# The seven-term product of the second pass over pairs of batches

## The chip, the cores and the metric

The kernel runs on one core of a Trainium2 chip. The core has a matrix engine, TensorE (PE; its weight loads are shown apart as PEld), and VectorE (DVE), ScalarE (ACT), GpSimd (POOL) and SyncE (SP, which issues nearly all transfers). The metric is the device time of one execution in microseconds, lower is better.

## The reference

Two stages follow each other. The first is attention over 8 batches of 8 heads, with 512 local tokens (each sees the tokens within 32 places, and all global ones) and 32 global tokens (each sees all). The second is a feed-forward block over the 8 x 544 token rows that come out of it:

```
h = x @ w_in                                  # x: 4352 x 512, w_in: 512 x 2048
sp = np.maximum(h, 0.0) + np.log1p(np.exp(-np.abs(h)))
g = h * erf(sp)
return (g @ w_out).astype(np.float32)         # w_out: 2048 x 512
```

## The kernel before

The hidden width of 2048 doesn't fit the on-chip memory at once, so the block runs in two passes of 1024 hidden columns each. Pass one stores its part of each product with w_out (`part`); pass two adds it (tile `pr`) to its own. A pass goes through nine chunks of tokens: chunks 0 to 7 are the 512 local tokens of a batch, chunk 8 all 256 global tokens. `ORDER` (L61) has the order: in pass two 7, 0, 1, ..., 6, 8, chunk 7 first, since its x stays from pass one.

**Numbers in two parts.** Every float32 operand is split into a high and a low part (names ending in h and l: `xh`/`xl`, `winh`/`winl`, `gh`/`gl`). A product is three matmuls: high by high, high by low, low by high. A split is a rounding copy (high part) and a subtraction (low part).

**A chunk.** `fetch_x` loads x from DRAM into `rx`, of which there is one buffer. The splits make its parts. A product with w_in gives h in the PSUM tile `h`, which is copied to `hs`. `gate` (L1185) takes four `hs` tiles at a time: on ACT a table load, four softplus, a table load and four erf (both into `sp`); then, per tile, sp times hs, the rounding copy `gh` and the subtraction `gl`. There are five buffers each of `gh` and `gl`. `project` (L1230) multiplies these by w_out into four PSUM tiles `op`; the result plus `pr` goes to `os` (two buffers) and out.

**The seven-term product.** In pass two, chunks 0 to 6 don't compute x @ w_in directly. `seven_x` (L1060) and `quad` (L1108) take it as a product of 2 x 2 blocks and need seven block products in place of eight (the scheme of Strassen and Winograd). Here the token dimension is halved: a block of x has 256 tokens of one batch, so each matmul has 256 columns. The block sums of w_in (`s0` to `s3`) are made once in pass two by `sums` (L1016); four sums of blocks of x, t1 to t4, are made for every batch, in `tx`. The `plus` steps on DVE (L1141) build two `hs` tiles out of the seven products: one copy and seven additions of 256 columns, from PSUM. Two products share a PSUM bank.

**The order of the work.** All of it is recorded as operations with a key, and `Program.schedule` (L147) plans them: it goes through a model of the engines, takes the lowest key that is ready, chooses among the engines that an operation allows, and so fixes the order of the instructions on each engine. The numbers at L30 to L36 and L64 set the keys. On the chip each engine runs its instructions strictly in that order. PSUM holds two `h` banks and six `a` banks; the latter hold the `op` tiles and every second `h` bank of a seven-term product.

Of the kernel before, what the change touches and what calls it, by code (L numbers as in the profile page):

```python
# [11 lines left out]
F32 = mybir.dt.float32  # L12
# [8 lines left out]
P = 128  # L21
# [10 lines left out]
QLEAD, VLEAD, RLEAD, XLEAD = (2.5517, -0.209), (2.5481, -1.9553), -1.589, (0.7497, -0.3176, 3.5675)  # L32
GOFF, POFF = (2.9757, 11.7735, 13.7388), (4.2669, 10.7934, 9.0092)
WIN, WOUT = (-7.7104, -6.1993, 11.4311, 3.451), (12.8759, 6.0818, 5.4762, 5.2864)
LATE = (59.1852, 78.8604, 52.8757, 44.675, 64.9113, 64.4638, 52.382, 80.1539)
BIAS, AHEAD = 0.8855, 14.1627  # L36

HARM = 1.719
# [19 lines left out]
MLEAD = 0.8021  # L58

SPAN = 7  # L60
ORDER = ((0, 1, 2, 3, 4, 5, 6, 8, 7), (7, 0, 1, 2, 3, 4, 5, 6, 8))  # L61
PLAIN, MERGE = 0, 0
SEVEN = (0, 1, 2, 3, 4, 5, 6)
SUMS = (84.0754, 85.2555)  # L64

TURN, GTURN = 22, 6
GSPLIT = 3
# [244 lines left out]
def kernel(  # L312
# [795 lines left out]
    def quad(c, q, X, key):  # L1108
# [47 lines left out]
        plus(3, [], ((1, L), 0, (1, L)))  # L1156
        return list(zip(H, S))

    def unit(ps, c, v, X, key):
# [24 lines left out]

    def gate(ps, c, us, key, first):  # L1185
# [10 lines left out]
        add(  # L1196
            {"ACT": 2.5 + 1.29 * (ps == 0) + 1.12 * len(us)},
            key,
            erf,
            [TAB, *(x[0] for x in us)],  # L1200
            [x[1] for x in us],
        )
        G = []
        for v, (Hb, SPb) in zip(first, us):
            nm = f"{ps}_{c}_{v}"
            k = key + 0.01 * v
            GH = mbuf([P, SL], F32R, f"gh_{nm}", "gh", 5)
            GL = mbuf([P, SL], F32R, f"gl_{nm}", "gl", 5)
            add({"DVE": 0.62, "POOL": 1.35}, k, lambda e, SPb=SPb, Hb=Hb: vec[e].tensor_tensor(SPb.ap, SPb.ap, Hb.ap, ALU.mult), [Hb], [SPb])
            add({"DVE": 0.35, "ACT": 0.56}, k, lambda e, SPb=SPb, GH=GH: copy(e, GH.ap, SPb.ap), [SPb], [GH])  # L1210
            add({"DVE": 0.62, "POOL": 1.35},
                k,
                lambda e, SPb=SPb, GH=GH, GL=GL: vec[e].tensor_tensor(GL.ap, SPb.ap, GH.ap.bitcast(F32), ALU.subtract),
                [SPb, GH],
                [GL],
            )
            G.append((GH, GL))
        return G

    def store_out(c, t, O):  # L1220
        if c < B:
# [8 lines left out]
    def project(ps, c, G, key, order=range(NU), OP=None, final=True):  # L1230
        nt = 4 if c < B else 2
        fresh = OP is None
        if fresh:
            OP = [psum_a([P, DM], f"op_{ps}_{c}_{t}") for t in range(nt)]

        def mm2(t, u):
            WH, WL = W["out", ps, u]
            for a in range(2):
                GH, GL = G[2 * u + a] if c < B else G[u]
                s0 = P * t + (0 if c < B else 256 * a)  # L1240
                lh, ll = (g.ap[:, s0 : s0 + P] for g in (GH, GL))
                first = fresh and u == order[0] and a == 0
                last = final and u == order[-1] and a == 1
                pe(OP[t].ap, lh, WH.ap[:, a, :], start=first, stop=False)
                pe(OP[t].ap, lh, WL.ap[:, a, :], start=False, stop=False)
                pe(OP[t].ap, ll, WH.ap[:, a, :], start=False, stop=last)

        for t in range(nt):
            if c == B:
# [67 lines left out]
    for ps in range(2):  # L1317
        for c in ORDER[ps]:
            n = NV if c < B else NU
            if ps == 1 and c == SPAN:  # L1320
                for i in range(5, 2 * NU):
                    load_late(i)
                for u in range(2):
                    sums(u, SUMS[u])
            if ps == 1 and c in SEVEN[PLAIN:]:
                X = seven_x(c, s - XLEAD[2])
                G = {}
                for i in range(0, NU, 2):
                    us = [x for q in range(i, i + 2) for x in quad(c, q, X, s + 2 * q)]
                    vs = [v for q in range(i, i + 2) for v in (q, q + NU)]  # L1330
                    G.update(zip(vs, gate(ps, c, us, s + 2 * i + 4 + GOFF[2], vs)))
                project(ps, c, G, s + 4 + POFF[2], (0, 2, 1, 3))
                s += n
                continue
            span = c == SPAN
            X = kept[0] if span and ps else load_x(ps, c, s - XLEAD[ps])
            us = [unit(ps, c, v, X, s + v) for v in range(n)]
            last = ps == 1 and c == ORDER[1][-1]
            G = []
            for a, z in ((0, 2), (2, 3), (3, 4)) if last else [(i, i + 4) for i in range(0, n, 4)]:  # L1340
                G += gate(ps, c, us[a:z], s + z + GOFF[ps], range(a, z))
            OP = project(ps, c, G, s + 4 + POFF[ps], range(NU), kept[1] if span and ps else None, not span or ps == 1)
            if span:
                kept = X, OP
            s += n
# [84 lines left out]
```

## Time and profile before

| | |
|---|---|
| Median of 3 runs | 903.62 us (903.03 to 903.79) |
| The profiled execution, its own time | 905.85 us |
| Its span (first to last instruction) | 904.0 us, so 1.85 us lie around it |
| PE busy | 891.8 us (99%), 9289 matmuls |
| DVE / ACT / POOL busy | 674.5 us (75%) / 522.2 us (58%) / 244.2 us (27%) |
| Pass two | from about 504 us to the end |

A matmul in flight overlaps the next one, and its end is modelled. So a busy PE says only that PE had work, and what a matmul costs is read from a long unbroken run of them: the time from the first start to the next piece's start, over the count. The granted clock of TensorE is 1.00 all through, its level of 2.4 GHz.

### The profile page before, as it was taken

The page shows a single profiled execution, that of the slowest core. Times are in us where ns is not written, and L with a number is a line of the kernel's source. Part 1 is how long each engine was busy: PE and PEld are TensorE (multiplying, and loading weights), DVE is VectorE, ACT ScalarE, POOL GpSimd, SP SyncE. Part 2 cuts the span into 40 slices and gives each one's busy share as a digit, 9 for nine tenths or more (in the row PEclk, how much of TensorE's full clock was granted, in tenths as well). Part 3 has the DMA queues.
Part 4 walks back from the last instruction along what each step waited for, and adds up shares of the span by engine and source line. Part 5 has one row for each costly group of instructions (what it writes and reads, how often), then busy time and mean ns, then how long its engine had stood idle before and what let it go on. Part 6 is the DMA issues. An engine that isn't in the chain of part 4 may idle for free.

```text
span 904.0 us, 22910 instructions
## 1 busy us (share of the span) xinstructions
PE 891.8 (99%) x9289; PEld 736.2 (81%) x9300; DVE 674.5 (75%) x1567; ACT 522.2 (58%) x962; POOL 244.2 (27%) x181
## 2 busy tenths in 40 slices
PE   9999999999999999999999999999999999999998
PEld 5677777777777777778898888988999899999986
DVE  3899797667757676773985898898878787787553
ACT  4778882855557466663756664655454545453540
POOL 0002242312533115330510324354222323233100
PEclk9999999999999999999999999999999999999999
DMA  9997988889798898975452210321324152303034
GB/s 349 349 314 232 301 256 241 303 242 319 261 257 276 252 307 269 278 239 164 131 136 95 115 47 1 71 63 33 70 71 94 57 115 60 96 24 95 1 94 116
DMA packets 93209, 153.53 MB, mean 170 GB/s; under 512 B 11952, under 2 KB 55728, under 8 KB 93104
## 3 DMA queue, kind: packets, MB, share of 16 engines
q1 hardware_dynamic: 92912, 151.81, 53.9%
q8 instruction: 73, 1.20, 0.6%
q10 hardware_dynamic: 192, 0.26, 0.1%
q14 instruction: 32, 0.26, 0.1%
HBM read 111.41 MB, written 40.63 MB: 168 GB/s over the span
## 4 chain that ended last, share of the span: by engine, by line
PE 80%; DVE 12%; DMA 4%; issue 2%; ACT 1%; POOL 1%; SPq 0%; DVEq 0%; POOLq 0%
PE op L350 34%; PE h L350 32%; PE s L350 5%; DVE raw_in L371 2%; PE o L350 2%; PE spare L350 2%; PE ga L350 2%; DMA rx<-xsc 2%; DVE xl L371 2%; DVE hs L371 1%; PE go L350 1%; PE s L351 1%; DVE gl L371 1%; DVE xh L371 1%; DVE sp L371 1%
## 5 line engine op out<-in xcount | busy, mean ns | idle before, releaser
L350 PE MATMUL op<-wouth,gh 128*128 128x512 f32 x544 | 217.5, 400 | 0.6 <-issue 0.6
L350 PE MATMUL op<-woutl,gh 128*128 128x512 f32 x544 | 212.4, 390 | 0.0
L350 PE MATMUL op<-wouth,gl 128*128 128x512 f32 x544 | 212.1, 390 | 0.0
L371 POOL TENSOR_TENSOR sp<-sp,hs 128x512 f32<-128x512 f32 x78 | 113.0, 1471 | 271.6 <-ACT sp L352 271.6
L350 PE MATMUL h<-xh,winh 128*128 128x512 f32 (+1 forms) x464 | 164.6, 355 | 0.6 <-DVE hs L371 0.5
L350 PE MATMUL h<-xh,winl 128*128 128x512 f32 (+1 forms) x464 | 162.2, 350 | 0.0
L350 PE MATMUL h<-xl,winh 128*128 128x512 f32 (+1 forms) x464 | 162.0, 349 | 0.0
L350 PEld LDWEIGHTS op<-wouth,gh 128*128 128x128 f32 x544 | 102.2, 188 | 27.3 <-issue 6.4
L350 PEld LDWEIGHTS op<-wouth,gl 128*128 128x128 f32 x544 | 102.1, 188 | 22.2
L350 PEld LDWEIGHTS op<-woutl,gh 128*128 128x128 f32 x544 | 102.3, 188 | 19.0 <-issue 0.5
L353 ACT ACT_TABLE_LOAD x90 | 115.5, 1283 | 2.3 <-PEq L1417 0.7
L352 ACT ACTIVATE gh<-sp 128x512 fp32r<-128x512 f32 x85 | 52.0, 631 | 92.8 <-PE op L350 84.4
L371 DVE TENSOR_TENSOR gl<-sp,gh 128x512 fp32r<-128x512 f32 x105 | 96.5, 939 | 7.2 <-ACT gh L352 6.4
L350 PEld LDWEIGHTS h<-xh,winh 128*128 128x128 f32 x464 | 87.7, 189 | 17.1 <-issue 2.7
L352 ACT ACTIVATE hs<-h 128x512 f32<-128x512 f32 (+1 forms) x68 | 36.9, 543 | 110.4 <-PE h L350 110.0
L350 PEld LDWEIGHTS h<-xl,winh 128*128 128x128 f32 x464 | 87.8, 189 | 12.0
L350 PEld LDWEIGHTS h<-xh,winl 128*128 128x128 f32 x464 | 87.7, 189 | 11.7
L371 DVE TENSOR_TENSOR hs<-h,hs 128x256 f32<-128x256 f32 x196 | 76.5, 417 | 11.8 <-PE h L350 7.7
L352 ACT ACTIVATE sp<-hs 128x512 f32<-128x512 f32 x136 | 74.9, 620 | 0.7 <-DVE gl L371 0.4
L352 ACT ACTIVATE sp<-sp 128x512 f32<-128x512 f32 x136 | 74.8, 620 | 0.4
L371 POOL TENSOR_TENSOR gl<-sp,gh 128x512 fp32r<-128x512 f32 x31 | 46.4, 1505 | 80.2 <-ACT gh L352 41.9
L371 DVE CAST gh<-sp 128x512 fp32r<-128x512 f32 x51 | 32.9, 652 | 43.2 <-PE op L350 42.8
(179 smaller groups left out, 1538.9 us busy)
## 6 DMA issues: line engine op xcount, KB each, us to landing
vb<-in_vB_dram SPq DMA_DIRECT2D x32, 650.0 KB, 5.7
qk<-in_qk_dram SPq DMA_DIRECT2D x30, 656.0 KB, 7.0
rx<-xsc SPq DMA_DIRECT2D x52, 256.0 KB, 5.2
va<-in_vA_dram SPq DMA_DIRECT2D x32, 390.0 KB, 5.8
px<-tp SPq DMA_DIRECT2D x84, 128.0 KB, 4.8
pt<-px SPq DMA_DIRECT2D x21, 512.0 KB, 5.5
raw_in<-in_w_in_dram SPq DMA_DIRECT2D x16, 512.0 KB, 7.3
xsc<-xT SPq DMA_DIRECT2D x32, 256.0 KB, 5.5
```

Source lines behind the costliest of these rows:

```text
L350: pe = lambda n, *a, **k: pinned(nc.tensor.matmul(n, *a, **k))
L351: tr = lambda *a, **k: pinned(nc.tensor.transpose(*a, **k))
L352: act = lambda *a, **k: pinned(nc.scalar.activation(*a, **k))
L353: table = lambda name: pinned(nc.scalar.preload_act_table_set(name))
L371: return lambda *a, **k: pinned(f(*a, **k))
```

## The change

In pass two chunks 1 and 2, 3 and 4, 5 and 6 are handled as three pairs; chunk 0 keeps the product over halves of its tokens. The new `ORDER` of pass two is 7, 8, 0, (1, 2), (3, 4), (5, 6): the global tokens come second, and the last chunk is a pair.

In a pair, the 2 x 2 blocks of x are the two batches by the two halves of the model dimension. So a block has 512 tokens, a matmul has 512 columns, and each product fills a PSUM bank by itself. `seven_pair` loads x in two steps, j = 0 and 1 (a quarter of the model dimension out of each of its halves, for both batches), into the single `rx` buffer with 16 transfers each; the differences are made in place there. `quad_pair` makes the seven products and adds them up: one copy and seven additions of 512 columns give four `hs` tiles, two for each batch.

`gate` gets a further argument: in a pair the rounding copies of a gate wait for the four `gl` of the gate before it, and the ACT part of the gates is kept in order (`TURNS`). The two gates of the pair's first batch stand ahead of the two of its second. Keys (`LATE`, `SUMS`, the new leads and offsets) are other numbers, and the gate of chunk 8 is no longer cut in three.

```diff
-ORDER = ((0, 1, 2, 3, 4, 5, 6, 8, 7), (7, 0, 1, 2, 3, 4, 5, 6, 8))
-SEVEN = (0, 1, 2, 3, 4, 5, 6)
+ORDER = ((0, 1, 2, 3, 4, 5, 6, 8, 7), (7, 8, 0, 1, 3, 5))
+SEVEN, PAIRS = (0,), (1, 3, 5)
...
+    def seven_pair(c, key):
...
+        for j in range(2):
+            k = key + 0.1 * j
+            RX = mbuf([P, 4 * SL], F32, f"rx_1_{c}_{j}", "rx", 1)
...
+                for h in range(2):
+                    src_ = xsc[c + h].rearrange("(i k a) d j x -> k j i d a x", i=2, k=2)[j]
+                    for g in range(4):
+                        for i in range(2):
+                            dst = RX.ap[WB * g : WB * g + WB, 2 * h + i, :].rearrange("p (a x) -> p a x", x=P)
+                            dma(dst, src_[g][i])
...
+            b11, b12, b21, b22 = block(0, 0), block(0, 1), block(1, 0), block(1, 1)
+            split_("11", b11)
+            diff(b12, b11, b11)
+            split_("21", b21)
+            split_("t1", b11)
+            diff(b22, b12, b12)
+            diff(b22, b11, b11)
+            split_("t2", b11)
+            split_("22", b22)
+            split_("t3", b12)
+            diff(b21, b11, b11)
+            split_("t4", b11)
+        return X
...
+    def quad_pair(c, q, X, key):
...
+        def product(i, a, x):
+            B_ = Buf(ps_h, [P, 2, 256], F32, f"h_1_{c}_{q}_{i}", "h", 2) if i % 2 == 0 else psum_a([P, 512], f"h_1_{c}_{q}_{i}")
...
+                    pe(flat(), wh, xh, start=(j == 0), stop=False)
+                    pe(flat(), wh, xl, start=False, stop=False)
+                    pe(flat(), wl, xh, start=False, stop=(j == 1))
...
+        b = product(0, "11", "11")
+        add({"ACT": 0.53, "DVE": 0.62}, key, lambda e, b=b: copy(e, C.ap, b[1]()), [b[0]], [C])
+        plus(1, product(1, "s2", "t2"), D, C)
+        plus(2, product(2, "12", "21"), C, C)
+        plus(3, product(3, "s1", "t1"), F, D)
+        plus(4, product(4, "s4", "22"), E, F)
+        b = product(5, "s3", "t3")
+        plus(5, b, F, F)
+        plus(5, b, D, D)
+        plus(6, product(6, "22", "t4"), D, D)
...
+            [TAB, *(x[0] for x in us), *([TURNS] if prev else [])],
+            [*(x[1] for x in us), *([TURNS] if ps else [])],
...
-            add({"DVE": 0.35, "ACT": 0.56}, k, lambda e, SPb=SPb, GH=GH: copy(e, GH.ap, SPb.ap), [SPb], [GH])
+            add({"DVE": 0.35, "ACT": 0.56}, k, lambda e, SPb=SPb, GH=GH: copy(e, GH.ap, SPb.ap), [SPb, *prev], [GH])
...
-            if ps == 1 and c in SEVEN[PLAIN:]:
-                X = seven_x(c, s - XLEAD[2])
+            if ps == 1 and c in PAIRS:
+                X = seven_pair(c, s - XPAIR)
...
+                for h in range(2):
+                    for n, us, vs in groups:
+                        G[h].update(zip(vs, gate(ps, c + h, us[h], s + GPAIR[h][n], vs, gated[-4:])))
+                for h in range(2):
+                    project(ps, c + h, G[h], s, (0, 2, 1, 3), keys=PPAIR[h])
```

What this does to the order of the instructions is seen at three places. The names in the rows: a tile, then its chunk and number, and at the end a buffer number.

PE, one product of the seven in the steady part of pass two. Before, the product with `s1` for batch 6 (`h_6_0_0` is its first bank, here the half on the right):

```order
L350 MATMUL h_6_0_0_10748<-xh_6_1_10667,s1h 128x256
L350 MATMUL h_6_0_0_10748<-xl_6_1_10691,s1h 128x256
L350 MATMUL h_6_0_0_10748<-xh_6_1_10667,s1l 128x256
L350 MATMUL h_6_0_0_10748<-xh_6_1_10667,s1h 128x256
L350 MATMUL h_6_0_0_10748<-xl_6_1_10691,s1h 128x256
L350 MATMUL h_6_0_0_10748<-xh_6_1_10667,s1l 128x256
```

Now the product with `s1` for batches 5 and 6 (bank `h_5_3_1`: pair 5, third index the product):

```order
L354 MATMUL h_5_3_1_10454<-xh_t_5_9922,s1h 128x512
L354 MATMUL h_5_3_1_10454<-xl_t_5_9939,s1h 128x512
L354 MATMUL h_5_3_1_10454<-xh_t_5_9922,s1l 128x512
L354 MATMUL h_5_3_1_10454<-xh_t_5_9922,s1h 128x512
L354 MATMUL h_5_3_1_10454<-xl_t_5_9939,s1h 128x512
L354 MATMUL h_5_3_1_10454<-xh_t_5_9922,s1l 128x512
```

Six matmuls of 512 columns stand where two batches took six of 256 each. Over the program PE has 504 rows fewer (4916 for 5420).

PE at the start of pass two, behind the first three tiles of chunk 7's product with the first quarter of w_out. Before, the fourth tile and then chunk 0:

```order
L350 MATMUL op_7_3_7808<-wouth_0_7147,gh_7_1_8017 128x512
L350 MATMUL op_7_3_7808<-woutl_0_7148,gh_7_1_8017 128x512
L350 MATMUL op_7_3_7808<-wouth_0_7147,gl_7_1_8039 128x512
L350 MATMUL h_0_0_0_8126<-xh_0_0_7683,winh_0_7077 128x256
L350 MATMUL h_0_0_0_8126<-xl_0_0_7689,winh_0_7077 128x256
```

Now the global tokens (`h_8`) follow the third tile:

```order
L354 MATMUL op_7_2_7782<-wouth_0_7077,gh_7_1_7987 128x512
L354 MATMUL op_7_2_7782<-woutl_0_7078,gh_7_1_7987 128x512
L354 MATMUL op_7_2_7782<-wouth_0_7077,gl_7_1_8008 128x512
L354 MATMUL h_8_0_8119<-xh_8_0_8080,winh_0_7326 128x256
L354 MATMUL h_8_0_8119<-xl_8_0_8098,winh_0_7326 128x256
```

The 96 matmuls of `h_8` and 24 of `op_7` now stand ahead of the first product of chunk 0, 120 rows further down than before.

SP, the loads of x in the steady part. Before (batches 2 and 3, four transfers each):

```order
L357 DMA rx_2_8578<-xsc_81 32x16x128 x4
L357 DMA out_dram<-os_7_2_8559 128x512
L357 DMA out_dram<-os_7_3_8586 128x512
L357 DMA rx_3_8967<-xsc_82 32x16x128 x4
L357 DMA pr_2_9120<-part_88 128x512
```

Now (second step of pair 3, both its batches):

```order
L361 DMA rx_3_1_9280<-xsc_82 32x4x128 x8
L361 DMA rx_3_1_9280<-xsc_83 32x4x128 x8
L361 DMA pr_2_9344<-part_88 128x512
L361 DMA pr_3_9346<-part_88 128x512
L361 DMA out_dram<-os_0_0_9309 128x512
```

Sixteen small transfers stand in one block, and the loads of `pr` and the stores are queued behind them.

## Rows read from the trace of the kernel before

**Rows 1.** The page, busy time: engine, busy us (share), instructions

```profile
PE 891.8 (99%) x9289; PEld 736.2 (81%) x9300; DVE 674.5 (75%) x1567; ACT 522.2 (58%) x962; POOL 244.2 (27%) x181
```

**Rows 2.** The page, chain that ended last: shares of the span by engine

```profile
PE 80%; DVE 12%; DMA 4%; issue 2%; ACT 1%; POOL 1%; SPq 0%; DVEq 0%; POOLq 0%
```

**Rows 3.** Stretches: length, busy us of PE, PEld, DVE, ACT, POOL, clock, DMA

```profile
560.00:575.00 15.00, 14.23 (x94) 12.79 (x92) 13.73 (x29) 10.25 (x16) 3.18 (x3) 1.00 0.43 92
600.00:620.00 20.00, 19.18 (x137) 17.47 (x136) 16.72 (x35) 13.38 (x22) 6.46 (x6) 1.00 0.39 106
687.02:729.02 42.00, 42.00 (x265) 38.17 (x264) 33.63 (x65) 21.30 (x36) 15.05 (x12) 1.00 0.31 76
863.06:899.82 36.76, 36.74 (x162) 30.06 (x161) 17.06 (x28) 9.56 (x11) 0.00 (x0) 1.00 0.39 115
899.82:904.00 4.18, 0.00 (x0) 0.00 (x0) 0.69 (x1) 0.00 (x0) 0.00 (x0) 0.97 0.50 126
```

**Rows 4.** The chain in order of time: start us, length us, what

```profile
687.18 5.03 PE h L350 x42
692.22 5.47 PE op L350 x24
...
863.06 36.76 PE op L350 x162
...
899.84 0.69 DVE os L371
```

**Rows 5.** Waits of PEld from 460 us on: us, times, longest

```profile
PEld h L350 <- DVE hs L371: 1.8, 3, 0.7
PEld h L350 <- DVE x L371: 0.7, 1, 0.7
PEld h L350 <- DVE xl L371: 0.5, 1, 0.5
```

**Rows 6.** Groups by shape, 645 to 813 us: count, busy us, mean ns, idle

```profile
L371 DVE TENSOR_TENSOR gl<-sp,gh 128x512 fp32r<-128x512 f32 x32 | 31.6, 994 | 0.1
L371 DVE CAST gh<-sp 128x512 fp32r<-128x512 f32 x22 | 17.3, 796 | 22.4 <-PE op L350 22.2
L371 DVE TENSOR_TENSOR tx<-rx 128x256 f32<-128x256 f32 x16 | 12.1, 794 | 0.0
L371 DVE TENSOR_TENSOR os<-op,pr 128x512 f32<-128x512 f32 x16 | 10.9, 684 | 2.0 <-DMA out_dram<-os 1.5 <-PE op L350 0.5
L371 DVE TENSOR_TENSOR tx<-rx,tx 128x256 f32<-128x256 f32 x8 | 3.0, 416 | 0.0
...
L371 POOL TENSOR_TENSOR sp<-sp,hs 128x512 f32<-128x512 f32 x30 | 43.9, 1491 | 108.6 <-ACT sp L352 108.6
...
L353 ACT ACT_TABLE_LOAD x16 | 20.5, 1283 | 0.3
L352 ACT ACTIVATE sp<-sp 128x512 f32<-128x512 f32 x36 | 19.8, 619 | 0.1
L352 ACT ACTIVATE gh<-sp 128x512 fp32r<-128x512 f32 x12 | 7.6, 633 | 32.3 <-PE op L350 32.1
```

**Rows 7.** Tile sp, 640 to 860 us: ns min/median/max, first and last start

```profile
L371 DVE TENSOR_TENSOR gl<-sp,gh x42: 676/684/1782, 645.4 to 857.3; 128x512 fp32r<-128x512 f32 x42
...
L371 DVE CAST gh<-sp x27: 417/482/1511, 644.8 to 855.7; 128x512 fp32r<-128x512 f32 x27
```

**Rows 8.** Tile rx from 500 us: issue, landing; the 1024 KB load from the page

```profile
L357 SPq DMA_DIRECT2D rx<-xsc x24: 318/487/489, 565.9 to 764.6; - x24
...
DMA to landing us min/median/max: 3.0/4.2/5.9
...
rx<-xsc SPq DMA_DIRECT2D x1, 1024.0 KB, 7.9
```

**Rows 9.** Stores, 870 to 896 us: landing; who waited, tile os, from 860

```profile
DMA to landing us min/median/max: 3.1/3.8/4.5
...
  DMA out_dram<-os: 5.4, 4
```

More of the change, by code (lines that the diff above doesn't have):

```diff
@@ L1157, in quad, with owner, fetch, diff @@
         return list(zip(H, S))
+    def seven_pair(c, key):
+        part = lambda: Buf(None, None, None, None, None)
+        X = {}
+        for n in ("11", "22"):
+            B_ = mbuf([P, 4 * SL], F32R, f"x_{n}_{c}", "raw", 2)
+            B_.view = [P, 4, SL]
+            X[n] = [(B_, 2 * i, [part(), part()]) for i in range(2)]
+        for n in ("t2", "21", "t1"):
+            X[n] = [(mbuf([P, 2 * SL], F32R, f"x{w}_{n}_{c}", f"x{w}", 3), 0, [part(), part()]) for w in "hl"]
+        for n, tags in (("t3", ("n", "ol3")), ("t4", ("ol2", "oh3"))):
+            X[n] = [
+                (Buf(wpool if t[0] == "o" else wb_pool, [P, 2 * SL], F32R, f"x{w}_{n}_{c}", t), 0, [part(), part()])
+                for w, t in zip("hl", tags)
+            ]
+        for n, two in X.items():
+            for B_, _, _ in two:
+                if n not in ("11", "22"):
+                    B_.view = [P, 2, SL]
+        begun = set()
+        def owner(b, p):
+            new = b not in begun
+            begun.add(b)
+            return ([], [b, p]) if new else ([b], [p])
+        for j in range(2):
+            k = key + 0.1 * j
+            RX = mbuf([P, 4 * SL], F32, f"rx_1_{c}_{j}", "rx", 1)
+            RX.view = [P, 4, SL]
+            RP = [part() for _ in range(4)]
+            def fetch(j=j, RX=RX):
+                for h in range(2):
[4 more added lines that the diff above has]
+                            dma(dst, src_[g][i])
+            add({"SP": 7.2}, k, fetch, [XSC[c + h, 2 * i + j] for h in range(2) for i in range(2)], [RX, *RP], moved=1700, issues=16)
+            k += STEP * 2
+            moved = lambda t: t.rearrange("p (a t q) -> p t a q", a=4, q=WB)
+            plain = lambda t: t.rearrange("p (t a q) -> p t a q", a=4, q=WB)
+            block = lambda i, h, RX=RX, RP=RP: (lambda: RX.ap[:, 2 * h + i, :], [RX, RP[2 * h + i]])
+            def diff(x, y, d, k=k):
+                add({"DVE": 0.65, "POOL": 1.4},
+                    k,
+                    lambda e: vec[e].tensor_tensor(d[0](), x[0](), y[0](), ALU.subtract),
+                    [*x[1], *y[1]],
+                    d[1][1:],
+                )
+            def split_(n, x, j=j, k=k):
+                (H, h0, HP), (L, l0, LP) = X[n]
+                hi = lambda: H.ap[:, h0 + j, :]
+                lo = lambda: L.ap[:, l0 + j, :]
+                reads, writes = owner(H, HP[j])
+                add({"DVE": 0.36, "ACT": 0.6}, k, lambda e: copy(e, plain(hi()), moved(x[0]())), [*reads, *x[1]], writes)
+                reads, writes = owner(L, LP[j])
+                add({"DVE": 0.65, "POOL": 1.4},
+                    k,
+                    lambda e: vec[e].tensor_tensor(plain(lo()), moved(x[0]()), plain(hi()).bitcast(F32), ALU.subtract),
+                    [*reads, *x[1], H, HP[j]],
+                    writes,
+                )
+            b11, b12, b21, b22 = block(0, 0), block(0, 1), block(1, 0), block(1, 1)
[11 more added lines that the diff above has]
+        return X
@@ new lines, in quad_pair, with run, plus @@
+    def quad_pair(c, q, X, key):
+        u, col = divmod(q, 2)
+        M0, M1 = W["in", 1, u], W["in", 1, 2 + u]
+        A = {"11": (M0, 0), "12": (M0, 1), "22": (M1, 1), **{f"s{n + 1}": (SUM[n], u) for n in range(4)}}
+        rows = (q, q + NU)
+        H = [mbuf([P, SL], F32, f"hs_1_{c}_{v}", "hs", 7) for v in rows]
+        far = ("hx", "hs", "hs", "hs", "hx", "sp", "sp", "hx")
+        many = {"hs": 7, "sp": 7, "hx": 3}
+        R = [Buf(wb_pool if far[v] == "hx" else mp, [P, SL], F32, f"hs_1_{c + 1}_{v}", far[v], many[far[v]]) for v in rows]
+        def product(i, a, x):
+            B_ = Buf(ps_h, [P, 2, 256], F32, f"h_1_{c}_{q}_{i}", "h", 2) if i % 2 == 0 else psum_a([P, 512], f"h_1_{c}_{q}_{i}")
+            if i % 2 == 0:
+                flat = lambda: B_.ap.rearrange("p a t -> p (a t)")
+            else:
+                flat = lambda: B_.ap
+            (WH, WL), w = A[a]
+            hi, lo = X[x]
+            def run():
+                for j in range(2):
+                    c0 = 256 * j + P * col
+                    wh, wl = (t.ap[:, w, c0 : c0 + P] for t in (WH, WL))
+                    xh, xl = (t.ap[:, n + j, :] for t, n, _ in (hi, lo))
+                    pe(flat(), wh, xh, start=(j == 0), stop=False)
+                    pe(flat(), wh, xl, start=False, stop=False)
+                    pe(flat(), wl, xh, start=False, stop=(j == 1))
+            deps = [WH, WL, *(b for t, _, parts in (hi, lo) for b in (t, *parts))]
+            add({"PE": 1.365}, key + 0.15 * i, run, deps, [B_], heat=3072, fetch=12)
+            return B_, flat
+        def plus(i, bank, d, x):
+            B_, flat = bank
+            add({"DVE": 0.65}, key + 0.15 * i, lambda: dve.tensor_tensor(d.ap, flat(), x.ap, ALU.add), [B_, x], [d])
+        (C, D), (E, F) = H, R
+        b = product(0, "11", "11")
[8 more added lines that the diff above has]
+        plus(6, product(6, "22", "t4"), D, D)
+        S = lambda n, v: mbuf([P, SL], F32, f"sp_1_{n}_{v}", "sp", 7)
+        return [[(t, S(c + h, v)) for t, v in zip(z, rows)] for h, z in enumerate((H, R))]
@@ L1183, in unit, with gate @@
         return Hb, SPb
-    def gate(ps, c, us, key, first):
+    def gate(ps, c, us, key, first, prev=()):
         def erf():
@@ L1214, in gate @@
                 [SPb, GH],
-                [GL],
+                [GL, gated[-1]],
             )
@@ L1228, in store_out, with project @@
             queue(out[n : n + SG, :], O.ap[SG * i : SG * i + SG, :])
-    def project(ps, c, G, key, order=range(NU), OP=None, final=True):
+    def project(ps, c, G, key, order=range(NU), OP=None, final=True, keys=None):
         nt = 4 if c < B else 2
@@ L1324 @@
                     sums(u, SUMS[u])
-            if ps == 1 and c in SEVEN[PLAIN:]:
-                X = seven_x(c, s - XLEAD[2])
+            if ps == 1 and c in PAIRS:
+                X = seven_pair(c, s - XPAIR)
+                G, groups = ({}, {}), []
+                for i in range(0, NU, 2):
+                    us = [[], []]
+                    for q in (i, i + 1):
+                        for h, two in enumerate(quad_pair(c, q, X, s + QUAD[q])):
+                            us[h] += two
+                    groups.append((i // 2, us, [v for q in (i, i + 1) for v in (q, q + NU)]))
+                for h in range(2):
[3 more added lines that the diff above has]
+                    project(ps, c + h, G[h], s, (0, 2, 1, 3), keys=PPAIR[h])
+                s += 2 * NV
+                continue
+            if ps == 1 and c in SEVEN:
+                X = seven_x(c, s - XLATE[1])
                 G = {}
@@ L1330 @@
                     vs = [v for q in range(i, i + 2) for v in (q, q + NU)]
-                    G.update(zip(vs, gate(ps, c, us, s + 2 * i + 4 + GOFF[2], vs)))
-                project(ps, c, G, s + 4 + POFF[2], (0, 2, 1, 3))
+                    G.update(zip(vs, gate(ps, c, us, s + 2 * i + 4 + GLATE[1], vs)))
+                project(ps, c, G, s + 4 + PLATE[1], (0, 2, 1, 3))
                 s += n
@@ L1335 @@
             span = c == SPAN
-            X = kept[0] if span and ps else load_x(ps, c, s - XLEAD[ps])
+            X = kept[0] if span and ps else load_x(ps, c, s - (XLEAD, XLATE)[ps][0])
             us = [unit(ps, c, v, X, s + v) for v in range(n)]
-            last = ps == 1 and c == ORDER[1][-1]
             G = []
-            for a, z in ((0, 2), (2, 3), (3, 4)) if last else [(i, i + 4) for i in range(0, n, 4)]:
-                G += gate(ps, c, us[a:z], s + z + GOFF[ps], range(a, z))
-            OP = project(ps, c, G, s + 4 + POFF[ps], range(NU), kept[1] if span and ps else None, not span or ps == 1)
+            for a, z in [(i, i + 4) for i in range(0, n, 4)]:
+                G += gate(ps, c, us[a:z], s + z + (GOFF, GLATE)[ps][0], range(a, z))
+            OP = project(ps, c, G, s + 4 + (POFF, PLATE)[ps][0], range(NU), kept[1] if span and ps else None, not span or ps == 1)
             if span:
```

22 lines of the change are left out of this document (14 added, 8 removed).

## The prediction, made before the changed kernel ran

> **What bounds the kernel now.** I read the page's busy times first: PE has work for 891.8 of 904.0 us [rows 1]. A busy share doesn't say that PE ends last, so the chain of waits comes second: 80% of the span is PE on the chain, DVE 12% [rows 2]. Third, the chain in order of time and the stretches: from 620 us to the last matmul the chain is PE alone, and it repeats. A batch of pass two is four quads of 42 matmuls with 256 columns and 96 projection matmuls with 512; the stretch 687.02 to 729.02 is one such batch, 264 matmuls (one more reaches in) in 42.00 us [rows 3]. In it the reader is to see PE busy 42.00 of 42.00 us, DVE 33.63. So there only PE's own work counts. The price of a matmul comes from the same views: the last 162, all of 512 columns, start within 36.76 us, 0.2269 us each [rows 3, 4]; 42 of 256 columns take 692.22 - 687.18 = 5.04 us, 0.1200 each [rows 4]. The whole batch confirms it: (42.00 - 96 x 0.2269) / 168 = 0.1203. Two matmuls of 256 columns therefore cost 13 to 14 ns more than one of 512. Fourth, what PE lost elsewhere in pass two: the waits of its weight loads add up to 3.0 us (1.8 + 0.7 + 0.5) [rows 5], and the two stretches in which PE isn't full, 560 to 575 and 600 to 620 us, are where chunks 0, 1 and 2 begin [rows 3].
>
> **The steady part.** Chunks 1 to 6 in pairs: a pair has 4 x 42 matmuls for the products and 2 x 96 for the projections, 360 of 512 columns, 360 x 0.2269 = 81.69 us. Before, two batches took 84.00. Three pairs: 3 x 2.31 = **6.9 us saved**. This holds as far as nothing makes PE wait; the clock is 1.00, the level of 2.4 GHz, with such matmuls back to back [rows 3], so I expect no change of it.
>
> The Trainium skill speaks against a gain of this size: "TensorE: Matmul & The Clock Gate", section "Back-to-back issue gap", gives a warm gap of columns / 2.4 + 2.5 ns for a matmul by itself, 109.2 ns for 256 columns and 215.8 for 512. By it the 504 pairs of matmuls would save 504 x 2.6 ns = 1.3 us, and the sum below would be 903.3. The rows differ: 120.0 and 226.9 ns, about 13 ns over the pure streaming time at either width, where the page has 2.5.
>
> **DVE, ACT and POOL in the steady part.** The volume of the splits and differences of x is the same. The additions become fewer and wider: 56 of 256 columns plus copies for two batches' four quads become 28 of 512. With 0.684 us for an addition from PSUM of that width (the row of `os`) they cost 19 us a pair. The order puts on DVE for pair 3: 28 such additions, 2 copies and 8 `os` (38 x 0.684), 15 `gl`, 13 sp times hs and 13 low parts of x (41 x 0.684 by the median of `gl`), 7 differences (14 x 0.416) and 11 rounding copies (0.417 the least): 64 us, in 81.7 of PE. With the durations that the trace has beside GpSimd's work (`gl` 0.994, copy 0.796, difference 2 x 0.794 [rows 6, 7]) it is 87 us. The first is nearer: the order has 3 to 8 GpSimd instructions a pair, where before one batch had 12 [rows 3]. So all of this lies beside PE, on average; what can break through is a chain at a place.
>
> **Place one: the start of a pair.** The x of pair 3 can't be split before the last quad of pair 1 frees the buffers. Take the end of that quad's first product as zero. PE then has 25 groups of six matmuls before it needs pair 3's first block: 25 x 1.361 = 34.0 us of cover. The chain against it: DVE's work up to the last use of the first step's x, 8 hs steps (5.5), 3 `gl` and 7 low parts (6.8), 1 copy (0.4), 3 differences (2.5) = 15.2 us; then 16 loads issued at 0.487 us each on SP = 7.8 and 4.2 to land [rows 8]; then a copy on ACT and a low part on DVE, 1.3. Sum 28.5 us, 5.5 inside the cover. With all DVE work at its duration beside GpSimd and the longest landing (5.9) it is 21.0 + 7.8 + 5.9 + 1.6 = 36.3, 2.3 late. A second chain runs to the projection of chunk 1 with its second group of `gh`: the same 15.2, a gate on ACT (two table loads and eight activations, 2 x 1.283 + 8 x 0.619 = 7.5 [rows 6]), sp times hs on POOL 1.5, three copies on ACT 3 x 0.633 = 1.9, a `gl` 0.7 = 26.8 against 21 groups, 28.6. At the slow durations 21.0 + 7.5 + 1.5 + 1.9 + 1.8 (the longest `gl` [rows 7]) = 33.7, 5.1 late. I take 0.5 us of wait per pair, 1.5 in all: both chains are inside at the median, the second by only 1.8; bounds 0 and 3 x 5.1. Behind SP's block of 16 stand `pr` loads and stores; they are needed 25 us later and hide.
>
> **Place two: the start of pass two.** Before, chunk 0's x was loaded long ahead; now chunk 8's x holds `rx` until the last product of chunk 7 frees the split buffers that chunk 8 needs, and DVE's next instruction is that split, so DVE waits there with the w_in sums queued behind it. From that product on: copies and low part of chunk 8, 2.1; a 1024 KB load, 7.9 with its issue 8.3 [rows 8]; then 12 DVE steps of 256 columns (5.0), 8 copies (3.3 at most), 5 steps of 512 (3.4): t2 is ready at 22.1 us. PE's cover is 18 + 24 projection matmuls (9.5), 96 of chunk 8 at 0.12 (11.5) and the first half of the bank (0.7): 21.8. t4 comes at 26.2 against 25.4. So 0.3 to 0.8 late at the median; with every DVE step at its slow duration 9.5 late. I take 1.5, near the median, a little for the six GpSimd instructions that the order has there. Against this stand the 3.0 us of waits before, which were these same starts and go. Waits after 1.5 + 1.5 = 3.0: **no difference**; bounds -3.0 and +22.
>
> The Trainium skill, "SBUF — State Buffer", section "Summary: rules for kernel authors", says that a VectorE instruction with two SBUF inputs and a GpSimd instruction that reads SBUF shut each other out whole. The trace agrees: `gl` takes 676 ns at the least and 1782 at the most. By the rule place two could lose up to the six GpSimd instructions, 6 x 1.49 = 8.9 us; an estimate, in the bound already.
>
> **The end.** Before, four 64 KB stores of chunk 8 follow the last addition: 4.18 us from the last matmul to the end [rows 3]. Now the last is one 256 KB store of chunk 6. Such stores land in 3.1 to 4.5 us, and with two `os` buffers the addition waits for the store two tiles before it (DVE waited 5.4 us for that in the last stretch [rows 9]): that store is issued some 3.4 us ahead of the last matmul (18 matmuls, 4.1 us, less the addition's 0.7), so 0.4 of wait are left at the median landing of 3.8; then 0.7 for the addition, 3.8 from issue to landing and 0.3 for the steps between: 5.2, **1.0 more**; bounds 0.2 and 2.2. 86 table loads in place of 90 are off the path.
>
> **Sum.** -6.9 + 0 + 1.0 = -5.9. The profiled execution took 905.85 (span 904.0 and 1.85 around it), so it would be 899.95; it lies 2.23 above the median of the runs, and the same step from the median gives 903.62 - 5.9 = **897.7 us**.
>
> **Rivals.**
> 1. No waits at all: the planner's chains hold and the 3.0 us go. 897.7 - 3.0 = 894.7. For it: 280 us without a wait before (620 to 899.8), and additions half as many. Against: place two has no margin.
> 2. The second step's load is the new wait: 2.3 us late at each pair in place of 0.5, and place two 4 in place of 1.5: +5.4 + 2.5 = 905.6 at worst, half of it 901.7. For it: four times the transfers on one queue. Against: DMA was busy for 30% in these stretches [rows 3]. Half of it is about the line between faster and no change.
> 3. A matmul of 512 columns with changing weights costs what the page's gap says relative to 256, saving 1.3: 903.3, no change. Against: pass one and every projection already change weights at each matmul, and the 162 in 36.76 us are of that sort.
> 4. Slower: the gates become the bound at the pairs' starts. A gate of the first batch must end before the second batch's begins, and five `gh` buffers bind it to PE; if POOL and DVE run at the slow durations, each pair waits 5.1 us: 897.7 - 1.5 + 15.3 = 911.5. It turns the change to slower than before from about 3.1 us late per pair on (897.7 - 1.5 + 3 x 3.1 = 905.5). Against: so few GpSimd instructions are left.
>
> **Chances.** Forecast 0.74, rival 1 0.08, rival 2 0.09 (half of it still faster), rival 3 0.02, rival 4 0.07. A measurement can tell about 0.2%, 1.8 us, from no change, so faster is below 901.8: 0.74 + 0.08 + 0.05 = 0.87; the same 0.04 + 0.02 = 0.06; slower 0.07. The forecast's own range, with waits of 1 to 6 and the end's bounds, is 895 to 901.3. The range, with rival 1 and part of rival 2, is 894.4 to 901.6.
>
> **What would show it.** Right: a quad of a pair takes 42 x 0.227 = 9.53 us in one piece, a pair 81.7 us with PE full, 504 matmuls fewer; waits of PE in pass two about 3 us, the largest at chunk 0's first products, on DVE; the tail near 5 us. Wrong: a quad of over 9.6 us without a wait (rival 3); waits on `xh_t` or `x` behind the second load at the pairs (rival 2), on `gh` or `gl` (rival 4).

## The result, and the profile after

The changed kernel took 894.21 us (median of 4 runs, 893.22 to 895.02) against 903.59 us before on the same chip: a ratio of 0.9897, 95% interval 0.9880 to 0.9914. Measured a second time it was 895.82 against 903.65 us, 0.9909 (0.9892 to 0.9927). So it is faster by some 8 to 9 us; 5.9 were forecast, and 894.21 lies 0.2 us below the range, which began at 894.4.

The page after, busy time: engine, busy us and share, instructions. It answers to [rows 1].

```profile
PE 882.5 (99%) x8785; PEld 709.3 (79%) x8796; DVE 655.5 (73%) x1481; ACT 516.3 (58%) x935; POOL 184.3 (21%) x134
```

Next, its chain by engine, which answers to [rows 2]: DVE's 12% has become 1%. Don't read that as 11% saved: in most of the span a chain can be followed back through an engine that was as nearly late as PE.

```profile
PE 91%; DMA 4%; ACT 2%; DVE 1%; issue 1%; SPq 0%; DVEq 0%; ACTq 0%
```

The stretches that answer to [rows 3] (columns as there): the two starts that were not full before, one pair, the last 36.76 us of matmuls, the tail.

```profile
560.00:575.00 15.00, 15.00 (x113) 14.39 (x112) 14.07 (x29) 9.31 (x15) 4.18 (x3) 1.00 0.29 102
600.00:620.00 20.00, 20.00 (x90) 16.56 (x89) 17.27 (x25) 12.10 (x19) 9.61 (x7) 1.00 0.26 80
645.00:726.70 81.70, 81.70 (x362) 67.66 (x361) 61.14 (x93) 41.85 (x63) 12.50 (x8) 1.00 0.23 71
852.29:889.05 36.76, 36.76 (x163) 30.11 (x161) 17.20 (x28) 16.69 (x26) 0.00 (x0) 1.00 0.28 86
889.05:893.23 4.18, 0.01 (x1) 0.00 (x0) 0.69 (x1) 0.00 (x0) 0.00 (x0) 0.99 0.33 125
```

PE is full all through the pair's stretch. It was laid 81.70 us long after the forecast, so its length proves nothing; a pair's 360 matmuls take 81.60 us from start to start (0.2267 each), where two batches took 84.00. The tail is 4.18 us, as before. PE's only wait in pass two stands in two lines, one as a wait of the weight load, one of the matmul; they are the same stop, from 622.3 us on (this view has who waited for whom, us, times, longest). It answers to [rows 5].

```profile
PEld h L354 <- ACT hs L356: 1.3, 1, 1.3
PE h L354 <- ACT hs L356: 0.9, 1, 0.9
```

To compare pass two by itself I count from the start of one and the same projection matmul of chunk 7, around 488 us, to the start of the last matmul, and from there to the end of the span. Whole executions differ by some 4 us. The start of that matmul in pass one, which the change doesn't touch, came between 485.9 and 491.3 us in the 13 traces. Pass two repeats much better (waits are what PE's starts show over their regular spacing; a sum over the starts that are late; "the clock's share" is what matmuls at a lower granted clock lost behind a wait, see the last section):

| kernel | pass two to the last matmul, us | of it waits | from there to the end |
|---|---|---|---|
| before, first / second trace | 409.11 / 408.11 | 2.9 / 1.9 | 4.6 / 4.7 |
| after, first / second trace | 400.09 / 400.09 | 1.1 / 1.1 | 4.6 / 4.5 |
| after with halves of 256 columns | 406.99 | 0.95 | 4.5 |
| after, pairs undone | 406.37 | under 0.4 | 7.3 |
| before, order alone changed | 410.12 | 3.9 with the clock's share | 7.2 |
| after with two pairs | 404.41 | 3.0 | 7.1 |
| after, four products moved off GpSimd | 398.94 | 0 | 4.65 |
| after, 32 loads for 16 | 421.64 | 22.5 with the clock's share | 4.6 |
| after, all products of the gates on GpSimd | 404.45 | 5.4 with the clock's share | 4.5 |
| after, last tile in halves | 400.10 | 1.1 | 4.1 |
| after, both last edits | 398.94 | 0 | 4.1 |

### The profile page after: what moved, and what is told of

The parts are those of the page before. It is cut to its first block, busy times and chain, and to the rows that moved or that the text cites. A ratio compares the mean times of both kernels' runs of the same rounds, so it can differ in the third digit from the quotient of the medians.

```text
span 893.2 us, 21849 instructions
## 1 busy us (share of the span) xinstructions
PE 882.5 (99%) x8785; PEld 709.3 (79%) x8796; DVE 655.5 (73%) x1481; ACT 516.3 (58%) x935; POOL 184.3 (21%) x134
## 4 chain that ended last, share of the span: by engine, by line
PE 91%; DMA 4%; ACT 2%; DVE 1%; issue 1%; SPq 0%; DVEq 0%; ACTq 0%
PE op L354 41%; PE h L354 38%; PE s L354 4%; PE o L354 2%; PE ga L354 1%; PE spare L354 1%; PE go L354 1%; DMA raw_in<-in_w_in_dram 1%; PE s L355 1%; DMA rx<-xsc 1%; ACT sp L356 1%; ACT L357 1%; DMA out_dram<-os 1%; DMA va<-in_vA_dram 1%; DMA xsc<-xT 1%
## 5 line engine op out<-in xcount | busy, mean ns | idle before, releaser
L354 PE MATMUL h<-xh,winh 128*128 128x512 f32 (+1 forms) x392 | 146.7, 374 | 0.0
L354 PE MATMUL h<-xh,winl 128*128 128x512 f32 (+1 forms) x392 | 144.5, 369 | 0.0
L354 PE MATMUL h<-xl,winh 128*128 128x512 f32 (+1 forms) x392 | 144.2, 368 | 0.0
L375 POOL TENSOR_TENSOR sp<-sp,hs 128x512 f32<-128x512 f32 x46 | 71.2, 1562 | 237.9 <-ACT sp L356 197.3
L375 DVE TENSOR_TENSOR gl<-sp,gh 128x512 fp32r<-128x512 f32 x106 | 83.4, 806 | 14.4 <-ACT gh L356 11.0
L354 PEld LDWEIGHTS h<-xh,winh 128*128 128x128 f32 x392 | 73.9, 189 | 15.5 <-issue 3.3
L354 PEld LDWEIGHTS h<-xh,winl 128*128 128x128 f32 x392 | 73.9, 188 | 12.7
L354 PEld LDWEIGHTS h<-xl,winh 128*128 128x128 f32 x392 | 74.0, 189 | 11.9
L375 DVE TENSOR_TENSOR hs<-h,hs 128x512 f32<-128x512 f32 (+1 forms) x112 | 66.0, 616 | 17.3 <-PE h L354 13.3
L375 DVE TENSOR_TENSOR sp<-sp,hs 128x512 f32<-128x512 f32 x90 | 72.2, 834 | 4.0 <-ACT sp L356 3.7
```

The costliest lines, as they stand in the source:

```text
L354: pe = lambda n, *a, **k: pinned(nc.tensor.matmul(n, *a, **k))
L375: return lambda *a, **k: pinned(f(*a, **k))
```

## The experiments

**The two kernels again.** Both unedited.

> The changed kernel again, unedited, in five rounds, to size the gain more closely than 894.21 against 903.59. Sum by what its first trace shows: 6.9 us from the wider matmuls, 1.8 us from waits of PE in pass two (2.9 before, 1.1 after), 0.1 from the end: 8.8 us, ratio 0.9903. If something besides these is saved (the medians of the first runs say 9.4 us), the ratio stays at 0.9897 or below, and the trace must show it ahead of pass two or in the steady stretch. Theory: the rest is a difference between two executions (512-column matmuls started 0.2269 us apart in the trace of before and 0.2267 in that of after), so the ratio comes out at 0.990 +- 0.001 and the start spacing of matmuls varies from trace to trace.

> The kernel before, unedited, for a second trace of it. Theory: pass two is the same to 0.2 us from trace to trace (from a given matmul of chunk 7 to the start of the last matmul: 409.1 us in the first trace of before, 400.09 in both traces of the changed kernel) and what differs between executions, up to 2 us, lies in the attention of pass one. So the stretch reads 409.0 to 409.2 again, with waits of 2.9 us at the starts of chunks 0, 1 and 2. Rival: pass two itself varies by a microsecond, and the gain of 9.0 us read there is partly chance.

Measured: 0.9909 for the changed kernel; pass two 400.09 us again. Before's second trace read 408.11, not 409.1: two of its five waits were missing, those of 0.44 and 0.41 us at 616 and 619 us. So the 3.0 us of [rows 5] were one execution's; another had 1.9, and the expectation of a repeat to 0.2 us fell for before. By pass two and the tail together the gain is 9.1 us against the first trace of before and 8.1 against the second. The two timed comparisons, 9.4 and 7.8 us, lie around that, and their intervals hold it; nothing outside pass two is needed.

**Halves.** Each product matmul of a pair as two of 256 columns:

```
-                for j in range(2):
+                for z, j in ((z, j) for z in (slice(0, 256), slice(256, 512)) for j in range(2)):
...
-                    pe(flat(), wh, xh, start=(j == 0), stop=False)
+                    pe(flat()[:, z], wh, xh[:, z], start=(j == 0), stop=False)
```

> The changed kernel with each 512-column product matmul of a pair issued as two of 256 columns, in the same order of everything else (504 matmuls more). Theory, the width is the gain: the 504 come back at 13.7 ns each, 6.9 us, so about 901.0 us less what longer quads give the late chain at the first pair (up to 1.0): 900 to 901, ratio 0.997. Rival, the gain is in the fewer and wider additions on DVE and in the order: it stays at 894 to 895. Rival, the gap of a matmul by the Trainium skill (page TensorE: Matmul & The Clock Gate, 2.5 ns of fixed cost): 1.3 us come back, 895.5.

Measured: 901.68 us, 0.9982 (0.9972 to 0.9993); the quotient of the two ratios, 0.9982 / 0.9909, is 0.7% or 6.6 us (the medians are 5.9 apart). In the trace pass two is 6.9 us longer, 7.1 without the waits: 14 ns for each of 504 pairs of matmuls. The price shows in unbroken pieces of the chain: 0.2267 us a matmul in the changed kernel (first line), 0.1199 in halves (second):

```profile
642.90 13.60 PE h L354 x60
641.81 14.39 PE h L354 x120
```

The width is what the pairs gain; DVE had the same number of instructions in both.

**Order alone, and pairs undone.** One from each side. In the kernel before:

```
-ORDER = (..., (7, 0, 1, 2, 3, 4, 5, 6, 8))
+ORDER = (..., (7, 8, 0, 1, 2, 3, 4, 5, 6))
```

and in the changed one:

```
-ORDER = (..., (7, 8, 0, 1, 3, 5))
-SEVEN, PAIRS = (0,), (1, 3, 5)
+ORDER = (..., (7, 8, 0, 1, 2, 3, 4, 5, 6))
+SEVEN, PAIRS = (0, 1, 2, 3, 4, 5, 6), ()
```

> The kernel before with the order of pass two alone changed: global tokens second instead of last, no pairs, the same 256-column products. Theory, the order removes waits: chunk 0's first products then have chunk 8's matmuls as cover, so the three waits of 0.7, 0.4 and 0.1 us at 567 to 570 go, those at chunks 1 and 2 (0.45, 0.44, 0.41 and what follows them) partly stay: 901.8 to 903.2, 0.4 to 1.8 us faster than before. Rival, the waits go only because the pairs leave GpSimd and VectorE less to do: 903.6, no change. Rival, chunk 8 between breaks the early load of chunk 0's x: some us slower.

> The changed kernel without pairs: its order (global tokens second) and its tables of lead times, all seven chunks one at a time with 256 columns. Theory: PE's work is that of before (7.2 us back), the waits lie at the starts of the chunks, where each has the cover of one batch, and the end has the two waits for stores that the other kernels with a single chunk at the end show (7.1 to 7.2 us from the last matmul's start, against 4.6): 410 to 414 us from the matmul of chunk 7 to the start of the last, so all of the change's gain is in the pairs. Rival: the tables and the order alone take waits out: 407.3 us or less (PE's work with pairs plus 7.2 and hardly a wait).

Measured: the order alone is slower, 907.62 us, 1.0046 (1.0029 to 1.0062); PE waits 2.3 us at the start of chunk 1, and the clock falls behind it (last section). Pairs undone: pass two in 406.37 us with hardly a wait. My theory of waits at each start fell, the rival held: what the change brings beside the pairs (the new tables of lead times and keys with the new order, and the gate of chunk 8 in one piece) takes the waits out; the order with the old tables doesn't. No run separates these. Both kernels lose 2.6 to 2.7 us at the end. So without pairs the change gains nothing in all: 413.7 us with the tail, where the kernel before had 413.7 and 412.8; what the tables save at the starts, the end takes back. The additions of the last tiles show why; DVE, pairs undone (start, length, what, and in brackets the idle time ahead and who ended it):

```profile
890.86 0.69 DVE L375 TENSOR_TENSOR os<-op,pr 128x512 f32<-128x512 f32 x1 [6.41 <-PE op L354]
892.22 0.69 DVE L375 TENSOR_TENSOR os<-op,pr 128x512 f32<-128x512 f32 x1 [0.67 <-PE op L354]
895.34 0.69 DVE L375 TENSOR_TENSOR os<-op,pr 128x512 f32<-128x512 f32 x1 [2.42 <-DMA out_dram<-os]
898.06 0.69 DVE L375 TENSOR_TENSOR os<-op,pr 128x512 f32<-128x512 f32 x1 [2.03 <-DMA out_dram<-os]
```

and of the changed kernel:

```profile
882.29 0.69 DVE L375 TENSOR_TENSOR os<-op,pr 128x512 f32<-128x512 f32 x1 [3.76 <-PE op L354]
885.01 0.69 DVE L375 TENSOR_TENSOR os<-op,pr 128x512 f32<-128x512 f32 x1 [2.03 <-PE op L354]
887.73 0.69 DVE L375 TENSOR_TENSOR os<-op,pr 128x512 f32<-128x512 f32 x1 [2.03 <-PE op L354]
889.43 0.69 DVE L375 TENSOR_TENSOR os<-op,pr 128x512 f32<-128x512 f32 x1 [1.01 <-DMA out_dram<-os]
```

With single chunks the tiles end 1.36 us apart, six matmuls, and with two `os` buffers the third and fourth each wait for a store. In the pair's order three of the four end 2.72 us apart, and the stores keep up but for the last 0.37 us (from the last matmul's end at 889.06).

**Two pairs.** `SEVEN, PAIRS = (0, 5, 6), (1, 3)`, the order to match.

> The changed kernel with two pairs, (1, 2) and (3, 4), and chunks 5 and 6 one at a time with 256 columns. Theory, each pair is worth 168 x 14.2 ns = 2.4 us of PE's work: pass two is 2.4 us longer than with three pairs by its matmuls, plus what new waits the single chunks bring at their starts and at the end (before, with single chunks, 0.4 to 1.3 us at three starts, none at the others). Expected: 402.5 to 404.5 us from the matmul of chunk 7 to the start of the last, against 400.09. Rival, the gain doesn't come pair by pair: no change of that stretch, or the whole 7.2 us.

Measured: 404.41 us, 4.3 more: 2.4 of work, and 1.9 of new waits at the start of chunk 5, the first single one. One pair's share is as the width says, and the end falls back to 7.1 us.

**The one wait.** At 622.3 us PE stops for a bank that ACT has to empty. The chain in order of time leads back through ACT to DVE ("issue" is time in which the engine waited for nothing that the profile shows):

```profile
617.73 1.49 DVE x L375
619.23 1.44 DVE xh_t L375
620.66 1.70 DVE rx L375
622.37 0.02 issue
622.39 0.63 ACT xh_t L356
623.02 0.49 ACT hs L356
623.51 0.04 issue
623.56 3.02 PE h L354 x12
```

The copy `hs` that frees the bank stands on ACT behind a rounding copy `xh_t`, which waits 2.8 us for DVE's difference `rx`. DVE's four instructions ahead of that are slow, and just then GpSimd multiplies `sp` by `hs`, four times:

```profile
615.82 5.99 POOL L375 TENSOR_TENSOR sp<-sp,hs 128x512 f32<-128x512 f32 x4 [6.67 <-ACT sp L356]
```

```profile
616.15 1.64 DVE L375 TENSOR_TENSOR rx<-rx 128x512 f32<-128x512 f32 x1
617.72 1.51 DVE L375 CAST x<-rx 128x512 fp32r<-128x512 f32 x1
619.15 1.51 DVE L375 CAST xh_t<-rx 128x512 fp32r<-128x512 f32 x1
620.59 1.77 DVE L375 TENSOR_TENSOR rx<-rx 128x512 f32<-128x512 f32 x1
```

The edit, in short, runs these four products on VectorE, at their place in the program:

```
-vec[e].tensor_tensor(SPb.ap, SPb.ap, Hb.ap, ALU.mult)
+vec["DVE" if ps == 1 and c == 0 and v in (2, 3, 6, 7) else e].tensor_tensor(SPb.ap, SPb.ap, Hb.ap, ALU.mult)
```

> The changed kernel with four products sp times hs of chunk 0 (rows 2, 3, 6, 7) issued on VectorE instead of GpSimd, at the same place in the program; the matmuls stand as before. In the trace these four run on GpSimd from 615.8 to 621.8 us, and the four VectorE instructions beside them, which make the second step's x of the first pair, take 1.4 to 1.8 us instead of 0.4 to 0.7. Theory, GpSimd's port makes PE's one wait of pass two: VectorE's four take 2.1 us again, the wait of 1.0 + 0.1 us at 622.3 goes, 893.2, 0.9 to 1.1 us under the changed kernel. Rival, the splits are late by VectorE's volume: the four more products (2.7 us) put the wait to another product, time unchanged or up to 1 us more.

Measured: 893.51 us, 0.9885 (0.9869 to 0.9902); pass two 398.94 us without a wait, 1.15 less. The same four instructions in that kernel, with the products behind them:

```profile
616.01 0.69 DVE L375 TENSOR_TENSOR rx<-rx 128x512 f32<-128x512 f32 x1
616.62 0.42 DVE L375 CAST x<-rx 128x512 fp32r<-128x512 f32 x1
616.95 0.42 DVE L375 CAST xh_t<-rx 128x512 fp32r<-128x512 f32 x1
617.29 0.68 DVE L375 TENSOR_TENSOR rx<-rx 128x512 f32<-128x512 f32 x1
617.89 1.28 DVE L375 TENSOR_TENSOR sp<-sp,hs 128x512 f32<-128x512 f32 x2
```

VectorE does its own work and GpSimd's four products sooner than its own work beside them. The cause is shown in the traces: the wait stands in both traces of the changed kernel and in that with the last tile in halves, and it is gone in both with these four products moved. The timed runs alone don't show it, as the intervals of the two ratios overlap.

**Rivals 2 and 4 by overload.** The pairs' loads in twice as many pieces, and the gates' products of chunks 1 to 6 all on GpSimd:

```
-                            dma(dst, src_[g][i])
+                            for z in (slice(0, 2), slice(2, 4)):
+                                dma(dst[:, z], src_[g][i][:, z])
```

```
+vec["POOL" if ps == 1 and 1 <= c <= 6 else e].tensor_tensor(SPb.ap, SPb.ap, Hb.ap, ALU.mult)
```

> The changed kernel with each of the 16 loads of 64 KB of a pair's step issued as two of 32 KB: 16 more issues, some 7.4 us more on SP ahead of each step's x. It measures how far rival 2 of the prediction was (a second step's load that comes late). Theory, the margins read from the trace: the first pair is already 1.0 us late, the second has 0.8 to 4.1 us, the third 3.2 to 7.9, so about 6 us at the first, 3.3 to 6.6 at the second and 0 to 4.2 at the third: PE waits 9 to 17 us in all. Rival, the loads have slack that the margins don't show (SP issues them long before the buffers' first use by DVE): at most 2 us more than the 1.1 us of wait now.

> The changed kernel with all products sp times hs of chunks 1 to 6 (48 of them) issued on GpSimd, at the same places in the program; 8 of them are there now. It measures rival 4 of the prediction (GpSimd and VectorE shut each other out, and the gates come late at the pairs' starts, 5.1 us a pair). Theory: 40 more GpSimd instructions of 1.3 to 1.7 us each hold up VectorE's instructions with two SBUF inputs beside them, and where the margin at the starts is 0.8 to 4 us, PE waits 3 to 15 us in all. Rival: VectorE is freed of 40 x 0.68 us and has room between the starts, so waits stay at 1 to 2 us.

Measured: with 32 issues pass two is 21.5 us longer. Some 16 us of the 22.5 are waits, inside the 9 to 17 that theory gave; some 6.5 stand behind four of them, where matmuls ran at a lower clock (last section), which theory had left out. So the loads are close to the path: 7.4 us more of issue break all three starts. With the products on GpSimd it is 4.4 us longer, all at the second pair (0.5 and 2.0 us of wait from 703 to 705 us, and the clock behind them). Of the starts that hold in the changed kernel, that is the one with the least margin, 0.8 us between the end of `xl_t` of t2 and its matmul; the third pair has 3.2 and holds.

**The end.** The last tile, summed and stored in two halves of 256 columns, on SP's and ACT's queues, from a free buffer; by itself and with the edit above.

```
-            O = mbuf([P, DM], F32, f"os_{ps}_{c}_{t}", "os", 2)
+            end = ps == 1 and c == 6 and t == 3
+            O = mbuf(..., "hs", 7) if end else mbuf(..., "os", 2)
...
+                    for z in (slice(0, 256), slice(256, 512)):
+                        ...
+                        queue = dma if z.start == 0 else (lambda *a: pinned(nc.scalar.dma_start(*a)))
```

> The changed kernel with the edit at the end alone (the last tile in two halves, on two queues, from a free buffer). Theory: the stretch to the start of the last matmul is 400.09 us as before; from there to the end 3.6 to 4.2 us against 4.5. Rival: a second store costs more than it saves, 4.5 us or more.

> The changed kernel with both edits: the four products of chunk 0 on VectorE, and the last tile of chunk 6 summed and stored in two halves of 256 columns, on two queues, from a buffer that is free (so that its addition waits for no earlier store). From the traces: PE's only wait of pass two goes (1.1 us, as the kernel with the first edit alone showed), the addition starts 0.37 us earlier, and the last 128 KB should land no later than the 256 KB did (3.1 us); an addition of half the width takes 0.41 us, and the first half's store overlaps the second half's addition. Theory: 400.09 - 1.15 = 398.94 us from the matmul of chunk 7 to the start of the last, and 3.6 to 4.2 us from there to the end, against 4.5; 0.4 to 1.0 us under the first edit alone, about 892.8 us, ratio 0.987 to 0.989. Rival: the landing has a fixed length and two queues don't shorten it, so only the 0.37 us of wait go.

Measured: 4.1 us from the start of the last matmul to the end against 4.5, in both. That is the 0.37 us of wait for a buffer and little else, so the rival fits as well as the theory: the halves landed in 1.7 and 1.8 us, and the whole tile had taken 2.0. With both edits pass two has no wait; 893.05 us, 0.9894 (0.9874 to 0.9913). By the traces it is 1.6 us under the changed kernel, which the timed runs, with a spread of 3 us, don't resolve.

## Why the prediction was off, point by point

Of the 3.5 us between 897.7 and 894.21 two terms make 3.0: "**no difference**" for the waits, which was 1.9 us off, and "**1.0 more**" at the end, which was 1.1 off. The mechanism of the gain itself, the width, was right.

- **Width, 6.9 us saved:** right, 7.1 measured. A pair takes 81.60 us where 81.69 were worked out; the price of 0.2269 came from a stretch that runs to the modelled end of the last matmul, and between starts it is 0.2267. Rival 3 is refuted: the halves gave back about 7 us, not 1.3. The gap that the Trainium skill gives (page "TensorE: Matmul & The Clock Gate", section "Back-to-back issue gap") is for a matmul by itself, and it doesn't carry over to this stream, in which every matmul has a weight load of its own (8785 matmuls and 8796 loads on the page).
- **DVE's volume beside PE:** right: 61.1 us in the 81.7 of a pair against 64 by the median durations.
- **Place two, 1.5 us of wait:** wrong; none came. The step that failed is "a 1024 KB load, 7.9 with its issue 8.3". The row is of a load that ran among three of 512 KB and a store of 256 KB, with the DMA engines busy nearly all the time (99.8% in the 10 us from 492 us). In its new place it runs beside two of 256 KB and lands in 5.5 us. The queue before, from 492 to 502 us (packets, MB, share of the engines), then the queue and the load now, from 558 to 565:

```profile
q1 hardware_dynamic: 1300, 3.47, 99.8%
q1 hardware_dynamic: 583, 1.16, 51.3%
rx<-xsc SPq DMA_DIRECT2D x1, 1024.0 KB, 5.5
```

  t2 was then ready 3.0 us ahead of its matmul, not 0.3 to 0.8 us late. The need had been placed rightly: at 21.9 us after the last product of chunk 7 (21.8 forecast); ready it was at 18.9 (22.1). 2.4 of these 3.2 us are the load. The Trainium skill, page "DMA: Bandwidth & Descriptors", section "Issuing engines are not separate DMA queues", says that DMAs issued from different engines end up on the same 16 DMA engines and interleave, and the two durations agree with that: what a load costs depends on what else moves. No run changed the other transfers alone, so this cause is argued from the two rows.
- **Place one, 0.5 us a pair:** the sum was near (1.1 for 1.5), but by luck: the place and the cause were others. Two pairs have no wait. The first stops by a chain that neither of my two sums had: ACT's queue, where the copy that empties PE's bank stands behind a copy that waits for DVE, which GpSimd holds up. Of the loads, the 64 KB ones landed in 2.0 us by the median, where I had taken 4.2.
- **"No difference" between 3.0 us of waits before and 3.0 after:** the step that cost most. After were 1.1; before were 2.9 in the trace used and 1.9 in the next. The kernel with pairs undone shows that the rest of the change takes the starts' waits out without the pairs. I had put new waits in their place: at place two by the price of a load that didn't hold, at the pairs as an allowance, though both chains there were inside their cover at the median.
- **The end, 1.0 us more:** wrong, 0.1 less. The wait of the last addition was 0.37 us as forecast (0.4). What failed is "3.8 from issue to landing and 0.3 for the steps between", 4.1 us in all: the last store has the DMA engines to itself and lands in 2.0 us, and 3.1 us after the end of the addition all is over. It is the quickest of the eight stores from 860 us on:

```profile
DMA to landing us min/median/max: 2.0/2.8/3.4
```

  The mechanism itself is real, and bigger than I had it where tiles end 1.36 us apart: 2.6 to 2.7 us.
- **The sum:** 897.7 - 1.9 (waits) - 1.1 (end) - 0.2 (width) = 894.5, against 894.21 and 895.82. The upper end of the forecast's own range, with waits of 6 us and an end of 2.2, adds up to 901.9 and not 901.3; nothing hangs on it.
- **Rivals:** it went nearest to rival 1, but its 894.7 is close by luck: the 1.1 us of wait that were left and the 1.1 us by which the end was too dear cancel. Rival 2's mechanism is 0.8 us of margin away at the second pair and 3.2 at the third; its price left out the clock, which added 1.5 us to a wait of 2.3 in the kernel with the order alone changed. Of rival 4, VectorE's slow durations beside GpSimd show at the first pair, but on the splits of x, not on a gate.

## What to carry to other kernels

A matmul of half the columns costs more than half (here 120 ns for 227): measure the surcharge from starts in a saturated stretch and multiply. For a transfer or a store that moves to a quieter place, take the duration from a quiet row, not the nearest by name; and for waits at a few starts, take more than one trace before you call them the cost. A second stream of work on GpSimd was no relief where VectorE's chain was the late one. A copy that frees a PE bank should perhaps not stand in a queue behind one that may wait; no run here moved that copy.

## What the runs showed of the hardware

PE's clock falls behind some waits, and that costs most of a short wait again: 1.4 to 1.7 us each in the six cases of these traces, behind waits of 2.0 to 3.9 us. In the kernel with the order alone changed PE had next to nothing for 2.4 us; then 3.2 us ran at a granted clock of 0.50, the level of 1.2 GHz (256 columns every 213 ns instead of 120), and then it was back:

```profile
613.00:615.40 2.40, 0.26 (x2) 0.04 (x1) 2.38 (x7) 1.78 (x4) 0.03 (x1) 0.98 0.00 0
615.40:618.60 3.20, 3.20 (x15) 3.20 (x16) 3.20 (x5) 1.65 (x4) 3.07 (x2) 0.50 0.44 164
618.60:622.00 3.40, 3.40 (x30) 3.40 (x30) 3.26 (x9) 3.29 (x6) 0.00 (x0) 0.98 0.59 138
```

16 matmuls at 93 ns more are 1.5 us for a wait of 2.3. In the kernel with 32 loads the stretches behind four waits read 0.52 to 0.76, and behind one of 3.2 us (from 709 us on) it stayed at 1.00, so not every wait of that length brings it. With the gates' products on GpSimd it read 0.58 behind the 2.0 us at 705 us. The stop of 1.0 us in the changed kernel didn't bring it. No run here shows what decides between them.

GpSimd also holds up VectorE's rounding copies, which read one tensor: 1.51 us beside it, 0.42 without. The rule as my prediction quoted it speaks only of instructions with two SBUF inputs, though [rows 7] had a copy of one tensor at 1511 ns. The Trainium skill, page "VectorE: DVE Perf Modes", section "Mode 2×_2P — use both read ports for one tensor", has a copy of one tensor read through both ports. These rows fit that, if GpSimd needs one of the two ports; they don't show the port itself.
